# A decode step in one kernel: the last K ahead of two V, and W_o cut in other sets

## The chip, the cores and the metric

The kernel runs on one core of a Trainium2 chip. The metric is the device time of one execution in microseconds; the figure for a kernel is the median of several runs. The program works on five engines: TensorE (PE), VectorE (DVE), ScalarE (ACT), GpSimd (POOL) and SyncE (SP), which here issues the transfers. Sixteen DMA engines carry these transfers.

## The reference

One decode step for two sequences: attention over a cache of 8192 positions with 32 heads, then a gated feed-forward block, each behind a layer norm and with a residual sum.

```python
def _A_ref(x, k_cache, v_cache, wq, wo):
    q = (x @ wq).reshape(B, Sq, Hq, Dh).transpose(0, 2, 1, 3)
    scores = jnp.einsum("bhqd,bhkd->bhqk", q, k) * (Dh ** -0.5)
    p = softmax(scores, axis=-1)
    o = jnp.einsum("bhqk,bhkd->bhqd", p, v)
    return o.transpose(0, 2, 1, 3).reshape(B, Sq, Hq * Dh) @ wo

def _B_ref(x, W_gate, W_up, W_down):
    gate, up = x @ W_gate, x @ W_up
    return (gate * (gate > 0) * up) @ W_down

h = x + _A_ref(_layernorm(x), k_cache, v_cache, wq, wo)
h2 = h + _B_ref(_layernorm(h), W_gate, W_up, W_down)
```

B = 2, Sq = 1, D = 512, Hq = Hkv = 32, Dh = 128, 8192 cached positions, F = 1376, all bf16. The two caches are 128 MB each and are read once.

## The kernel before

**Steps.** The work runs in 32 steps; step i takes one sequence b and a group g of two heads. Each step loads 4 MB of K into one half of `kbuf` and 4 MB of V into one half of `vbuf` (half i % 2). A partition holds 128 positions of one head, partitions 0 to 63 head 0 and 64 to 127 head 1. In the text "K 31" is the K of step 31, and so on; the last step, 31, is called L in the changed code.

**Order by hand.** The whole kernel is in one manual schedule: each engine runs its instructions in program order, and waits are put in where a region of a buffer is still read or written. This holds for SP's queue of transfers too: a load that waits holds back every load behind it. Waits go by regions, so that a quarter of V can be issued when the matmuls that read that quarter are done. There are eight semaphores for transfers, used in turn: a transfer waits until the one eight places before it has landed.

**Scores.** In a step the 128 positions of a partition are shared out. VectorE takes 96 of them (80 in the last step): `products` (L338) multiplies K by q in place, `scores` (L353) adds halves down to a width of 8 and reduces (L357), then takes the maximum of a partition (L361). TensorE takes the other 32 (48 in the last step): `scores_pe` transposes eight tiles at a time (L311), ScalarE copies them out as `kT` (L313), and matmuls with q (L302) gather rows, which are copied (L318), transposed back (L321) and put into `scol` (L328). `largest` (L368) takes the maximum over partitions by a matmul, and `exponentials` (L380, L383) writes the weights into `pgz` and their sums into `zc`.

**Values.** `values(i, part)` multiplies the weights by V, 16 matmuls of 128x512 in each of two parts (L399), copies the result (L406), and where a group of heads ends, gathers it as `o_ps` (L411). `values_cols` does the same with V as the stationary operand (L423), 128 small matmuls. `sums`, `shares` and `normalise` divide by the sums of the exponentials and write `ocol`.

**Output projection.** W_o is 4 MB, in `wbig` behind the place of wq. Heads 0 to 26 are taken in three sets (`SETS`: first head, heads, partitions, place), loaded such that each partition holds whole rows of W_o: 16 heads and 8 heads on 128 partitions, 3 heads on 48. `spread` (L437, L442) lays the heads' outputs over these partitions, `attend_set` turns them into rows with `rest` (L456) and multiplies (L464). The last five heads go one by one with `attend` (L472), their W_o laid out by d. The set of 3 heads is loaded by two transfers of 24 partitions each, whose rows are named in the order `[[r*D, 6], [6*r*D, 4]]`. `spread` runs when a group of heads is finished: sets 0, 1 and 2 in steps 25, 29 and 31.

**The end.** After the loop come the last sums, `values_cols(31)`, five heads of `attend`, the residual sum `hc` (L541), the second layer norm, gate and up (L561) with weights that lie in `kbuf`'s first half, where K 30 was, and W_down (L588), whose chunks 0 to 7, 10, 8 and 9 are used in that order. The loads of gate, up and W_down are the last on SP's queue, behind the four quarters of V 31.

**Order of the last loads:** K 29, V 28, K 30, V 29, K 31, V 30, V 31 in four quarters, gate, up, W_down in three.

## Time and profile before

| | us |
|---|---|
| median of 3 runs | 665.12 (664.72 to 666.16) |
| the profiled execution | 664.74 |
| its span | 663.0 |
| TensorE busy | 489.4 (74%) |
| VectorE busy | 475.9 (72%) |
| ScalarE busy | 219.5 (33%) |
| transfers on SP's queue | 98.6% of 16 engines' span |

The profile is of one execution, and times in it count from the start of its span; the execution took 1.74 us more than the span. Three groups of instructions show what the engines wait for (name, count, busy time, mean of one in ns, then the idle time just before and what ended it):

```
L399 PE MATMUL pv_ps<-vbuf,pgz 128*8 128x512 bf16 x960 | 277.6, 455 | 66.6 <-DMA vbuf<-in_A_v_cache_dram 66.6
L338 DVE TENSOR_TENSOR kbuf<-kbuf,qrep 128x12288 bf16<-128x12288 bf16 (+1 forms) x32 | 208.8, 6525 | 107.9 <-DMA kbuf<-in_A_k_cache_dram 107.9
L313 ACT ACTIVATE kT<-t_ps 128x1024 bf16<-128x1024 bf16 x130 | 129.4, 1022 | 43.0 <-PE t_ps L311 40.9
```

Both TensorE and VectorE wait for V and K. A step lasts 19.4 us, two loads of 9.7 us.

### The profile page before, as it was taken

How to read it: one execution, taken by the hardware profiler on the slowest of the kernel's cores; microseconds unless marked ns; L12 is line 12 of the kernel's file. 1: busy time of each engine (PE TensorE's matmuls, PEld its weight loads, DVE VectorE, ACT ScalarE, POOL GpSimd, SP SyncE). 2: the span in 40 equal slices, each digit the busy share in tenths (PEclk: the TensorE clock that was granted, in tenths of full speed). 3: DMA queues.
4: the chain of work that ended last, by engine and by line, in shares of the span. 5: the costliest groups of instructions: out<-in, count | busy, mean ns of one | idle time of the engine just before them, and what ended most of it. 6: DMA issues, size and time to landing. Idle time of an engine off the chain costs nothing.

```text
span 663.0 us, 7717 instructions
## 1 busy us (share of the span) xinstructions
PE 489.4 (74%) x3282; PEld 229.2 (35%) x3282; DVE 475.9 (72%) x306; ACT 219.5 (33%) x400; POOL 17.8 (3%) x73
## 2 busy tenths in 40 slices
PE   3656777787777668787777867776877876788786
PEld 2422232333223333332333322333333432343266
DVE  0594788667778777778877767877777787776771
ACT  1532233333233333133333322333331333332250
POOL 8200000000000000000000000000000000000000
PEclk9968878988878998787899877899887888987785
DMA  9999999999999999999999999999999999999995
GB/s 380 431 413 445 424 443 428 427 439 430 429 436 437 426 441 427 427 440 431 430 435 428 434 433 432 429 434 437 426 435 438 422 435 438 431 432 432 433 417 202
DMA packets 11970, 281.58 MB, mean 425 GB/s; under 512 B 1518, under 2 KB 2288, under 8 KB 2672
## 3 DMA queue, kind: packets, MB, share of 16 engines
q1 hardware_dynamic: 11932, 281.09, 98.6%
q8 instruction: 25, 0.41, 0.2%
q14 instruction: 9, 0.07, 0.0%
q10 hardware_dynamic: 4, 0.00, 0.0%
HBM read 281.09 MB, written 0.00 MB: 424 GB/s over the span
## 4 chain that ended last, share of the span: by engine, by line
DMA 68%; PE 21%; DVE 9%; ACT 1%; issue 0%; SPq 0%; DVEq 0%; ACTq 0%
DMA vbuf<-in_A_v_cache_dram 53%; PE pv_ps L399 17%; DMA kbuf<-in_A_k_cache_dram 15%; DVE kbuf L353 4%; DVE kbuf L338 4%; PE o_ps L423 1%; PE mx_ps L368 1%; ACT kT L313 1%; DVE scol L357 1%; PE row_ps L302 0%; PE g_ps L561 0%; PE t_ps L311 0%; PE d_ps L588 0%; PE u_ps L561 0%; PE z_ps L268 0%
## 5 line engine op out<-in xcount | busy, mean ns | idle before, releaser
L399 PE MATMUL pv_ps<-vbuf,pgz 128*8 128x512 bf16 x960 | 277.6, 455 | 66.6 <-DMA vbuf<-in_A_v_cache_dram 66.6
L338 DVE TENSOR_TENSOR kbuf<-kbuf,qrep 128x12288 bf16<-128x12288 bf16 (+1 forms) x32 | 208.8, 6525 | 107.9 <-DMA kbuf<-in_A_k_cache_dram 107.9
L353 DVE TENSOR_TENSOR kbuf<-kbuf 128x6144 bf16<-128x6144 bf16 (+4 forms) x128 | 211.1, 1649 | 4.2
L399 PEld LDWEIGHTS <-pgz 128*8 128x8 bf16 x960 | 92.4, 99 | 227.8 <-issue 153.5
L313 ACT ACTIVATE kT<-t_ps 128x1024 bf16<-128x1024 bf16 x130 | 129.4, 1022 | 43.0 <-PE t_ps L311 40.9
L383 ACT ACTIVATE pgz<-scol,nm 64x128 bf16<-64x128 f32 x64 | 25.5, 399 | 263.0 <-DVE nm L380 262.2
L302 PE MATMUL row_ps<-kT,qz 128*16 128x512 bf16 (+1 forms) x260 | 78.5, 383 | 40.1 <-ACT kT L313 37.4
L311 PE MATMUL t_ps<-ident,kbuf 128*128 128x128 bf16 x1040 | 77.6, 225 | 10.6 <-DMA kbuf<-in_A_k_cache_dram 10.3
L311 PEld LDWEIGHTS <-kbuf 128*128 128x128 bf16 x1040 | 61.4, 101 | 51.1 <-issue 30.6
L302 PEld LDWEIGHTS <-qz 128*16 128x16 bf16 (+1 forms) x260 | 20.0, 87 | 63.2 <-issue 47.0
L406 ACT ACTIVATE pv<-pv_ps 8x512 f32<-8x512 f32 x30 | 17.6, 588 | 65.7 <-PE pv_ps L399 65.7
L380 DVE TENSOR_REDUCE nm<-mx_ps 128x2 f32<-128x128 f32 x32 | 9.3, 292 | 37.8 <-PE mx_ps L368 37.8
L357 DVE TENSOR_REDUCE scol<-kbuf 128x96 f32<-128x768 bf16 (+1 forms) x32 | 30.4, 949 | 1.1
L321 PE MATMUL sc_ps<-ident_f,rows 16*128 16x16 f32 (+1 forms) x128 | 13.4, 214 | 21.6 <-ACT rows L318 21.6
L318 ACT ACTIVATE rows<-row_ps 16x512 f32<-16x512 f32 (+1 forms) x32 | 18.8, 586 | 21.8 <-PE row_ps L302 21.8
L368 PE MATMUL mx_ps<-nscale,pm 128*128 128x128 f32 x64 | 16.2, 337 | 9.7 <-DVE pm L361 9.5
L321 PEld LDWEIGHTS sc_ps<-ident_f,rows 16*128 16x128 f32 (+1 forms) x128 | 10.3, 136 | 37.7 <-ACT rows L318 37.7
L328 ACT ACTIVATE scol<-sc_ps 64x32 f32<-64x32 f32 (+1 forms) x64 | 14.2, 223 | 17.0 <-PE sc_ps L321 16.2
L368 PEld LDWEIGHTS mx_ps<-nscale,pm 128*128 128x128 f32 x64 | 9.9, 195 | 23.4 <-DVE pm L361 16.0
L411 PE MATMUL o_ps<-pick,pv 128*128 128x8 f32 (+1 forms) x64 | 8.4, 258 | 5.5 <-ACT pv L406 5.5
L383 ACT ACTIVATION_READ_ACCUMULATOR pgz<-scol,nm 64x1 f32 x64 | 11.8, 185 | 0.0
L361 DVE TENSOR_REDUCE pm<-scol 128x1 f32<-128x128 f32 x32 | 9.2, 286 | 3.4 <-ACT scol L328 0.2
(91 smaller groups left out, 107.7 us busy)
## 6 DMA issues: line engine op xcount, KB each, us to landing
kbuf<-in_A_k_cache_dram SPq DMA_DIRECT2D x32, 4096.0 KB, 24.3
vbuf<-in_A_v_cache_dram SPq DMA_DIRECT2D x31, 4096.0 KB, 29.4
wbig<-in_A_wq_dram SPq DMA_DIRECT2D x1, 4096.0 KB, 12.1
vbuf<-in_A_v_cache_dram SPq DMA_DIRECT2D x4, 1024.0 KB, 18.2
wbig<-in_A_wo_dram SPq DMA_DIRECT2D x1, 2048.0 KB, 31.7
kbuf<-in_B_W_gate_dram SPq DMA_DIRECT2D x1, 1376.0 KB, 21.4
kbuf<-in_B_W_up_dram SPq DMA_DIRECT2D x1, 1376.0 KB, 24.2
wbig<-in_A_wo_dram SPq DMA_DIRECT2D x1, 1024.0 KB, 33.8
```

The lines of the kernel that those rows point to most:

```text
L302: nc.tensor.matmul(out=row_ps, lhsT=qz[:, b, g, z0:z0 + 2 * U], rhs=kTs[c0][:, k * P:(k + 4) * P], start=(u == 0), stop=(u == U - 1),)
L311: nc.tensor.transpose(t_ps[:, k, :], kt[:, t * Dh:(t + 1) * Dh], ident)
L313: nc.scalar.activation(out=kTs[c0], in_=t_ps.rearrange("p t s -> p (t s)"), func=ACT.Copy)
L318: nc.scalar.activation(out=rows, in_=row_ps, func=ACT.Copy)
L321: nc.tensor.transpose(sc_ps[:, t].rearrange("p u j -> p (u j)"), rows[:, t * P:(t + 1) * P], ident_f[0:2 * U, 0:2 * U],)
L338: nc.vector.tensor_tensor(out=kv, in0=kv, in1=_free(qrep, (b * NG + g) * Dh, [[0, nv], [1, Dh]]), op=ALU.mult,)
L353: nc.vector.tensor_tensor(out=lo, in0=lo, in1=_free(kt, half, [[Dh, nv], [1, half]]), op=ALU.add,)
L357: nc.vector.tensor_reduce(out=scol[:, 0:nv], in_=_free(kt, 0, [[Dh, nv], [1, 8]]), axis=AXIS.X, op=ALU.add,)
L368: nc.tensor.matmul(out=mx_ps.rearrange("p a b -> p (a b)"), lhsT=_free(pms[i], 0, [[0, P]]), rhs=nscale, start=True, stop=True,)
L383: nc.scalar.activation(out=pgz[r, s, :, j, :], in_=scol[r, :].rearrange("p (u t) -> p u t", t=VG), func=ACT.Exp, scale=SCALE, bias=nm[r, j ...
L399: nc.tensor.matmul(out=pv_ps[i][r, :], lhsT=pgz[:, s, u].rearrange("p j t -> p (j t)"), rhs=vbuf[:, s, u * VG * Dh:(u + 1) * VG * Dh], sta ...
L406: nc.scalar.activation(out=pv[r, w], in_=pv_ps[i][r, :], func=ACT.Copy)
```

## The change

Three things, in one diff:

- **Order of the last loads.** V 29 is no longer issued in step 28 but in step 29 behind K 31, in two halves; the order becomes K 29, V 28, K 30, K 31, V 29 in two, V 30, V 31 in four, gate, up, W_down in three. The loop ends one step sooner, and the last step is written out.
- **TensorE's share of step 31 in two parts.** `scores_pe` takes a range of tiles. Its first three groups run in step 30 behind `scores(30)`, the other three between the two parts of `values(29)`. Steps 30 and 31 use `values_cols`, each behind the exponentials of step 31; single heads are attended between its pieces.
- **W_o in other sets.** 16 heads on 128 partitions; 4 heads on 32 partitions, by two transfers of 16 partitions with rows named in the order `[[r*D, 4], [4*r*D, 4]]`; 4 heads on 128 partitions, kept in `wd_sb` where W_down comes later; the last 8 heads by d. Sets 1 and 2 are both worked in step 29. The memset of the unused partitions of set 2 is gone, and the input row x is kept in another chunk of `wd_sb`.

```diff
-    SETS = [(0, 16, P, 0), (16, 8, P, 16), (24, 3, 48, 32)]
-    WO_T = 24
-    HM = 27
+    SETS = [(0, 16, P, 0), (16, 4, 32, 16), (20, 4, P, 0)]
+    WO_T = 32
+    HM = 24
...
+    def wo_set(k):
+        at = SETS[k][3] * D
+        return wd_sb.rearrange("p c n -> p (c n)")[:, at:] if k == 2 else wbig[:, at:]
...
-        xr = wd_sb[0:B, 0, :]
+        xr = wd_sb[0:B, FC - 2, :]
...
-        nc.gpsimd.memset(wbig[0:HALF, SETS[2][3] * D:(SETS[2][3] + SROWS[2]) * D], 0.0)
...
-            part, rows = (P, [[r * D, P]]) if w == P else (24, [[r * D, 6], [6 * r * D, 4]])
+            part, rows = (P, [[r * D, P]]) if w == P else (16, [[r * D, 4], [4 * r * D, 4]])
...
-        def scores_pe(i):
+        def scores_pe(i, c1, c2):
...
-            for c0 in range(0, npe, TPC):
+            for c0 in range(c1, c2, TPC):
...
+            if c2 < npe:
+                return
...
                     nc.vector.tensor_copy(
-                        _free(placed, b * HALF, [[32, 2], [1, 4], [4, 6]]), _free(sp, 0, [[24, 2], [6, 4], [1, 6]]),
+                        _free(placed, b * HALF, [[32, 2], [1, 4], [4, 4]]), _free(sp, 0, [[16, 2], [4, 4], [1, 4]]),
                     )
...
-        def attend_set(k, sps, last=False):
+        def attend_set(k, sps):
...
-            p1 = P if w == P else HALF
+            p1 = P if w == P else 48
...
+        L = N - 1
+        for i in range(L):
             if i >= 2:
                 sums(i - 2)
+            scores_pe(i, 0, NPE)
             products(i)
+            ready = behind(i - 2) if i >= 2 else []
+            for k, sps in ready:
+                attend_set(k, sps)
+            if 1 <= i < L - 1:
                 values(i - 1, 0)
             scores(i)
+            if i == L - 1:
+                scores_pe(L, 0, NPE_LAST // 2)
             largest(i)
             exponentials(i)
             if i + 2 < N:
                 load_kv(A_k_cache, kbuf, i + 2)
+            if i == L - 2:
+                load_kv(A_v_cache, vbuf, i, pieces=2)
+            if 1 <= i < L - 1:
                 values(i - 1, 1)
+            if i + 1 < L and i != L - 3:
+                load_kv(A_v_cache, vbuf, i + 1)
...
+        products(L)
+        values(L - 2, 0)
+        scores_pe(L, NPE_LAST // 2, NPE_LAST)
+        values(L - 2, 1)
+        load_kv(A_v_cache, vbuf, L, pieces=4)
...
+        sums(L - 2)
+        scores(L)
+        behind(L - 2)
+        largest(L)
+        exponentials(L)
+        values_cols(L - 1)
+        for h in range(HM, 2 * (NG - 2)):
+            attend(h)
+        sums(L - 1)
+        behind(L - 1)
+        values_cols(L, 0, NT // 4)
+        sums(L)
+        shares(L)
+        values_cols(L, NT // 4, NT // 2)
+        for h in range(2 * (NG - 2), 2 * (NG - 1)):
+            attend(h)
+        values_cols(L, NT // 2, NT)
+        normalise(L)
+        for h in range(2 * (NG - 1), Hq):
             attend(h)
```

More of the change, by code (lines that the diff above doesn't have):

```diff
@@ L217 @@
                 nc.scalar.activation(out=qrep[:, b, g0:g0 + 4, :], in_=r_ps, func=ACT.Copy)
-        for (h0, n, w, at), r in zip(SETS, SROWS):
-            part, rows = (P, [[r * D, P]]) if w == P else (24, [[r * D, 6], [6 * r * D, 4]])
-            for k in range(w // part):
+        for k, ((h0, n, w, _), r) in enumerate(zip(SETS, SROWS)):
+            part, rows = (P, [[r * D, P]]) if w == P else (16, [[r * D, 4], [4 * r * D, 4]])
+            for j in range(w // part):
                 nc.sync.dma_start(
-                    out=wbig[32 * k:32 * k + part, at * D:(at + r) * D],
-                    in_=_dram(A_wo, (h0 * Dh + part * k * r) * D, rows + [[1, r * D]]),
+                    out=wo_set(k)[32 * j:32 * j + part, 0:r * D],
+                    in_=_dram(A_wo, (h0 * Dh + part * j * r) * D, rows + [[1, r * D]]),
                 )
@@ L285, in share @@
             return NT - npe, npe
-        def scores_pe(i):
+        rows_pe = {}
+        def scores_pe(i, c1, c2):
             b, g = steps[i]
-            s = i % 2
-            kt = kbuf[:, s, :]
+            kt = kbuf[:, i % 2, :]
             nv, npe = share(i)
             U = npe // 4
-            row_ps = ps.tile([2 * U, 4 * P], f32, tag="row")
-            kTs = {}
+            if c1 == 0:
+                rows_pe[i] = (ps.tile([2 * U, 4 * P], f32, tag="row", name="row_ps"), {})
+            row_ps, kTs = rows_pe[i]
             def times_q(c0):
@@ L323, in scores_pe @@
                 )
-            scol = small.tile([P, NT], f32, tag="scol")
-            scols[i] = scol
+            scols[i] = small.tile([P, NT], f32, tag="scol", name="scol")
             for j in range(2):
@@ L328, in scores_pe @@
                 nc.scalar.activation(
-                    out=scol[r, nv:NT].rearrange("p (u t) -> p t u", t=4), in_=sc_ps[r, :, :, j], func=ACT.Copy,
+                    out=scols[i][r, nv:NT].rearrange("p (u t) -> p t u", t=4), in_=sc_ps[r, :, :, j], func=ACT.Copy,
                 )
@@ L430, in spread @@
         def spread(k):
-            h0, n, w, at = SETS[k]
+            h0, n, w, _ = SETS[k]
             nq = Dh // SROWS[k]
@@ L442, in spread @@
                     nc.vector.tensor_copy(
-                        _free(placed, b * HALF, [[32, 2], [1, 4], [4, 6]]), _free(sp, 0, [[24, 2], [6, 4], [1, 6]]),
+                        _free(placed, b * HALF, [[32, 2], [1, 4], [4, 4]]), _free(sp, 0, [[16, 2], [4, 4], [1, 4]]),
                     )
-                    sp = placed[:, b, :]
+                    sp = placed[:, b, 0:48]
                 sps.append(sp)
             return sps
-        def attend_set(k, sps, last=False):
-            h0, n, w, at = SETS[k]
+        def attend_set(k, sps):
+            w = SETS[k][2]
             r = SROWS[k]
-            p1 = P if w == P else HALF
+            p1 = P if w == P else 48
             or_ps = ps.tile([P, B, r], f32, tag="mx")
@@ L456, in attend_set @@
                 nc.tensor.matmul(out=or_ps[0:p1, b, :], lhsT=sps[b], rhs=rest[k], start=True, stop=True)
-            o, i = orow[k][0:p1], or_ps[0:p1].rearrange("p b c -> p c b")
-            if last:
-                nc.vector.tensor_copy(o, i)
-            else:
-                nc.scalar.activation(out=o, in_=i, func=ACT.Copy)
+            nc.scalar.activation(out=orow[k][0:p1], in_=or_ps[0:p1].rearrange("p b c -> p c b"), func=ACT.Copy)
             for c0 in range(r):
@@ L465, in attend_set @@
                         out=att_ps[:, c, :],
-                        lhsT=_free(wbig[0:p1], (at + c0) * D + c, [[KC, P]]), rhs=orow[k][0:p1, c0, :],
+                        lhsT=_free(wo_set(k)[0:p1], c0 * D + c, [[KC, P]]), rhs=orow[k][0:p1, c0, :],
                         start=(k == 0 and c0 == 0 and c == 0), stop=False, skip_group_check=True,
@@ L488, in behind @@
             return ready
-        for i in range(N):
-            last = i == N - 1
+        L = N - 1
+        for i in range(L):
             if i >= 2:
                 sums(i - 2)
-            scores_pe(i)
+            scores_pe(i, 0, NPE)
             products(i)
-            if i >= 2 and not last:
-                for k, sps in behind(i - 2):
-                    attend_set(k, sps)
-            if last:
-                values_cols(i - 1, 0, NT // 2)
-            elif i >= 1:
+            ready = behind(i - 2) if i >= 2 else []
+            for k, sps in ready:
+                attend_set(k, sps)
+            if 1 <= i < L - 1:
@@ L502 @@
                 values(i - 1, 0)
             scores(i)
+            if i == L - 1:
+                scores_pe(L, 0, NPE_LAST // 2)
             largest(i)
-            ready = behind(i - 2) if last else []
             exponentials(i)
-            if last:
-                values_cols(i - 1, NT // 2, NT)
-                for k, sps in ready:
-                    attend_set(k, sps, last=True)
             if i + 2 < N:
                 load_kv(A_k_cache, kbuf, i + 2)
-            if 1 <= i < N - 1:
+            if i == L - 2:
+                load_kv(A_v_cache, vbuf, i, pieces=2)
@@ L514 @@
+            if 1 <= i < L - 1:
                 values(i - 1, 1)
-            if i + 1 < N:
-                load_kv(A_v_cache, vbuf, i + 1, pieces=4 if i + 1 == N - 1 else 1)
+            if i + 1 < L and i != L - 3:
+                load_kv(A_v_cache, vbuf, i + 1)
             if i == NG // 2:
                 nc.sync.dma_start(out=wd_sb[:, FC - 1, :], in_=_dram(B_W_down, FSETS[-1][0] * D, [[D, P], [1, D]]))
-            if i == N - 2:
-                for w, src in ((0, B_W_gate), (1, B_W_up)):
-                    nc.sync.dma_start(
-                        out=wgu[:, w], in_=_dram(src, 0, [[KC * F, P], [F, KC], [1, F]]),
-                    )
-                for f0, n in FSETS[:-1]:
-                    nc.sync.dma_start(
-                        out=wd_sb[:, f0 // P:f0 // P + n, :],
-                        in_=_dram(B_W_down, f0 * D, [[n * D, P], [1, n * D]]),
-                    )
@@ L529 @@
-        sums(N - 2)
-        shares(N - 2)
-        normalise(N - 2)
-        sums(N - 1)
-        shares(N - 1)
-        values_cols(N - 1)
-        normalise(N - 1)
-        for h in range(HM, Hq):
+        products(L)
[3 more added lines that the diff above has]
+        load_kv(A_v_cache, vbuf, L, pieces=4)
+        for w, src in ((0, B_W_gate), (1, B_W_up)):
+            nc.sync.dma_start(out=wgu[:, w], in_=_dram(src, 0, [[KC * F, P], [F, KC], [1, F]]))
@@ new lines @@
+        for f0, n in FSETS[:-1]:
+            nc.sync.dma_start(
+                out=wd_sb[:, f0 // P:f0 // P + n, :], in_=_dram(B_W_down, f0 * D, [[n * D, P], [1, n * D]]),
+            )
+        sums(L - 2)
[11 more added lines that the diff above has]
+        shares(L)
```

## The prediction

> **What bounds the kernel.** I read the page first, then the tail in narrow stretches, then SyncE's issues, then the chain of waits.

> ```profile
> span 663.0 us, 7717 instructions
> ...
> DMA  9999999999999999999999999999999999999995
> ...
> HBM read 281.09 MB, written 0.00 MB: 424 GB/s over the span
> ```

> The DMA engines are full from start to end and the bytes are the same after the change (W_o is cut differently, 4 MB both times). So only the last stretch can move: how far the sixteen DMA engines end apart, and what is computed after.

> ```profile
> 650.00:652.00 2.00, 2.00 (x78) 2.00 (x75) 0.16 (x1) 0.00 (x0) 0.00 (x0) 0.50 0.92 387
> 652.00:653.00 1.00, 0.74 (x12) 0.66 (x10) 0.17 (x1) 0.00 (x0) 0.00 (x0) 0.50 0.81 326
> 653.00:654.00 1.00, 0.54 (x13) 0.47 (x14) 0.57 (x4) 0.00 (x0) 0.00 (x0) 0.50 0.78 305
> 654.00:655.00 1.00, 0.59 (x19) 0.51 (x17) 0.00 (x0) 0.00 (x0) 0.00 (x0) 0.50 0.62 251
> 655.00:656.00 1.00, 1.00 (x27) 1.00 (x26) 0.00 (x0) 0.00 (x0) 0.00 (x0) 0.50 0.48 174
> 656.00:657.00 1.00, 1.00 (x34) 1.00 (x35) 0.69 (x5) 0.00 (x0) 0.00 (x0) 0.50 0.08 33
> 657.00:658.00 1.00, 1.00 (x37) 1.00 (x35) 0.32 (x3) 0.00 (x0) 0.00 (x0) 0.50 0.06 23
> ```

> The last two columns are the DMA share and GB/s. The engines stop one after another from 651 on, and from 657 the share is 0.06, one engine of sixteen. This straggler carries the last of W_down. I followed every packet of the trace engine by engine (a packet starts where the last of its engine ends) and took the sixteen completions of each load. The last W_down load completes at 651.44 to 651.64 on three engines, 653.94 to 654.44 on three, 655.63 to 656.12 on eight, 656.59 on one, 658.44 on the straggler.

> ```profile
> 641.14 1.70 PE o_ps L423 x64
> ...
> 645.61 1.20 PE att_ps L464 x32
> ...
> 648.24 3.41 PE o_ps L423 x128
> ...
> 657.46 1.50 PE d_ps L588 x44
> 658.96 0.02 issue
> 658.98 0.17 DVE y L593
> ```

> The chain says PE, but d_ps reads chunks 8 and 9 last, and they land at 658.44: y starts 0.54 us later (eight matmuls at 1.50/44 = 0.034, and the way to VectorE). Computation and straggler end together; shortening one gains nothing.

> ```profile
> 604.11 0.33 SPq L126 DMA_DIRECT2D kbuf<-in_A_k_cache_dram  x1
> 610.18 20.37 SPq L126 DMA_DIRECT2D vbuf<-in_A_v_cache_dram  x5
> 630.65 0.38 SPq L521 DMA_DIRECT2D kbuf<-in_B_W_gate_dram  x1
> ```

> K 31 is issued at 604.11, V 30 at 610.18, the quarters of V 31 at 623.33, 626.26, 628.50 and 630.23, each as soon as the values matmuls on that quarter are done.

> **Part 1, the order.** V 29 (issued 589.62, landed 619.68) goes behind K 31 (landed 629.35). They swap places: K 31 lands near 619.7, V 29 near 629.3. No byte is added; one more issue, 0.33 us on SP, is hidden by its 14 us waits. What is late next is the queue: between K 30's issue (584.16) and K 31's nothing waits on SP. The earliest engines finish K 30 at 602.6, so they run dry for 3 to 4 us. They end 7 us ahead of the straggler, so that costs nothing; if they had no such lead it would cost those 3 to 4 us.

> **Part 2, step 31 earlier.** The transposes of step 31 (632.01 to 641.14 before) are split: three groups while VectorE is in step 30, three between the halves of values(29). That delays values(29,1) and so the last two quarters of V 31, on SP behind it; gate, up and down too. Working forward: largest(30) ends near 626; values(29,0) 16 matmuls, half at 0.43 and half at 0.22, to 631; the second half of the transposes 9.1 - 3 x 1.13 = 5.7 to 637; values(29,1) 16 x 0.22 to 640.5. The quarters are then issued by 629, 631, 639 and 640.5; engines at mid field want the third at 639 to 641, so at most some of them idle 1 us. VectorE: products(31) 5.5, tree 5.7 and reductions 1.1 end near 638.5; it then waits for o_ps(29) (copy 0.6, eight matmuls 1.05) to 642, so exponentials(31) end near 644.7, as before (644.9). From the tail goes set 2 (0.21 + 0.17 + 1.20 us) and 12 of 20 last matmuls (0.4). V 31's last quarter lands at 648.75 as before, and half of values_cols (64 x 0.027 = 1.7) comes behind it or behind PE: hc near 652.0 against 652.36. Gain of computation: 0.35 us.

> **Part 3, W_o.** Set 1 becomes 64 matmuls, set 2 sixteen, in place of 32: 48 x 0.0375 = 1.8 us on PE in step 29, and four more VectorE operations of 0.2 us, hidden by PE's waits for V (2.8 us) and VectorE's for K (3.1 us); uncovered, 2.6 us. K 31's issue moves by about 0.8 us, more if K 29 lands later. The POOL memset (3.50 us) goes; PE waits for wq until 12.9 anyway: nothing.

> The DMA side matters more. The two 192 KB loads with an outer count of 6 ran on six engines only: each completed on six, and their 8 KB packets went to six. The new loads have an outer count of 4: I take four engines. Time per engine, start to start: 16 KB 0.608, 8 KB 0.306, 4 KB 0.157, 1 KB 0.0437 us. Before, behind set 0: 8 x 0.306 + 40 x 0.0437 = 4.20 on all and 8 x 0.306 more on six, 6.65. After: 8 x 0.157 + 64 x 0.0437 = 4.06 on all, and 8 x 0.608 more on four, 8.92. So +2.27 us on four engines, -2.59 on an engine that drops out of the six, -0.14 on the rest. An engine never catches up, as its queue is hardly ever empty: the offsets of t = 54 are still there at the end.

> Is the straggler among the four? It is one of the six: its 16 KB instruction fetches at 131, 379 and 603 cost it about 1.2 us each. The fetches of 16 KB go around eight engines in a fixed order; the other seven are all outside the six. The 8 KB fetches sit on four others of the six, and the sixth has none. Two neighbouring blocks, five engines and then eight, fit this: the six are the first block and the first engine of the second, the straggler is the last of them, and the four leave it out. But the trace names no engine; the other end fits too. Bounds: left out, it ends at 658.44 - 2.59 = 655.85, and the engine at 656.59 is last with 658.86; kept, 660.71.

> [...]

> [...]

> **Sum.** Straggler left out: last landing 658.86, y 0.54 later: 659.40 against 658.98, +0.42. The profiled execution took 664.74 (span 663.0 and 1.74 around it), 0.38 under the median of 665.12. Forecast 665.12 + 0.4 = 665.5, own range 664.6 to 666.4.

> **Rivals.** (a) The straggler is one of the four: +2.27, 667.4. For it: the straggler is one of the six, and four of six are kept; against: the order of fetches. It decides as soon as that engine is among those four, since nothing else ends after 658.86.
> (b) PE is late. If the clock is halved through values(29), as in 618.8 to 625.6, 16 matmuls cost 16 x 0.21 = 3.4 us more in the second half, and o_ps(29), the exponentials and hc are late by that: hc 652.0 + 3.4 = 655.4 against 652.36, +3.0, 668.1; with the other half of the first too, 1.7 more, 669.8. It decides once hc is over 0.8 us later than the 652.0 above. For it: little work on PE at 623 to 625; against: the clock was full while transposes ran, 605 to 618.
> (c) The loads spread over all engines, or the straggler's helpers differ: 512 KB in 16 KB packets is two per engine, 1.22, so the six go by 4.06 + 1.22 - 6.65 = -1.37 and the rest by +1.08: last landing 657.2. Then computation decides: between -0.35 and -1.24, 664.3. For it: nothing but that the four are not shown.

> **Chances.** Forecast 0.52, (a) 0.24, (b) 0.14, (c) 0.10. About 0.2% (1.3 us) is what can be told from no change. Of the forecast 0.03 falls faster (it costs the spans by single rows, and computation may end earlier than I put it) and 0.03 slower, of (b) 0.02 within, of (c) half faster: faster 0.08, same 0.46 + 0.02 + 0.05 = 0.53, slower 0.03 + 0.24 + 0.12 = 0.39. Range: from (c) below to (a) and 0.4 us of its own spread above, 664.3 to 667.8; most of (b) stays out, about 0.12.

> **What would show it.** The products of K 31 should start near 626 and not 629.4; hc near 652; the DMA share should fall to about 0.06 to 0.2 after 656 and end near 658.5 if the forecast holds, near 660.4 under (a). Under (b) the values matmuls of step 29 after 632 take 0.43. If y starts more than 1 us after the last landing, computation bounds the end and my part 2 is wrong; if the loads of set 1 complete on sixteen engines, part 3 is.

## The result and the profile after

The changed kernel takes 666.76 us (median of 9 runs, 666.04 to 668.14), the kernel before 664.77 us beside it: a ratio of 1.0026, 95% interval 1.0015 to 1.0037, that is 2.0 us more. The profiled execution took 667.58 us, its span is 665.9. It is one of the longer of the nine, 0.82 us over the median, so the profile shows a larger loss (2.8 us against the 664.74 of the profiled execution before) than the medians do.

The page of the changed kernel: span, the DMA engines' busy tenths, the packets that carry instructions (count, MB, share of 16 engines), and the rate.

```profile
span 665.9 us, 7791 instructions
...
DMA  9999999999999999999999999999999999999995
...
q8 instruction: 26, 0.43, 0.2%
...
HBM read 281.09 MB, written 0.00 MB: 422 GB/s over the span
```

The bytes are the same and the engines are as full as before. The next view cuts the end into stretches (length, busy time and instructions of TensorE, its weight loads, VectorE, ScalarE and GpSimd, then the granted clock, the DMA share and GB/s).

```profile
652.00:653.00 1.00, 0.35 (x14) 0.26 (x10) 0.00 (x0) 0.00 (x0) 0.00 (x0) 0.50 0.96 402
653.00:654.00 1.00, 0.00 (x0) 0.00 (x0) 0.00 (x0) 0.00 (x0) 0.00 (x0) 0.50 0.99 407
654.00:655.00 1.00, 0.20 (x2) 0.15 (x3) 0.16 (x1) 0.00 (x0) 0.00 (x0) 0.50 0.94 387
...
656.00:657.00 1.00, 0.54 (x12) 0.47 (x12) 0.57 (x4) 0.00 (x0) 0.00 (x0) 0.50 0.94 367
657.00:658.00 1.00, 1.00 (x39) 1.00 (x36) 0.00 (x0) 0.00 (x0) 0.00 (x0) 0.50 0.40 160
658.00:659.00 1.00, 1.00 (x27) 1.00 (x24) 0.33 (x2) 0.00 (x0) 0.00 (x0) 0.50 0.12 47
```

Two things are to be seen. The DMA share falls in one cliff after 657 where it fell slowly from 651 on before: the engines now end together, and late. And from 653 to 654 no engine computes at all, TensorE included, though V 31 had landed at 649.61. The chain of waits says for how long (start, duration, what):

```profile
646.74 0.24 PE o_ps L431 x9
646.98 1.36 issue
648.35 0.78 PE o_ps L431 x23
...
650.67 1.68 PE o_ps L431 x63
652.35 2.19 issue
654.54 0.20 PE o_ps L431
...
655.42 0.18 DVE hc L556
...
656.70 1.47 PE g_ps L576 x44
...
659.92 1.48 PE d_ps L603 x44
661.43 0.17 DVE y L608
```

The kernel before had one such wait on its chain, which the prediction passed over; it also stands at number 6337:

```profile
653.63 0.69 PE g_ps L561 x17
654.32 0.41 issue
654.73 0.96 PE g_ps L561 x27
```

The sixteen completions of the last load of W_down, in order of time:

```
before   651.44 651.60 651.64 653.94 654.38 654.44 655.63 655.78 655.78 655.86 655.89 655.97 655.98 656.12 656.59 658.44
changed  656.93 656.96 656.99 657.09 657.12 657.16 657.20 657.44 657.74 657.85 657.92 658.36 658.40 658.67 658.92 659.27
```

The spread of 7.0 us has become 2.3, but the last is 0.83 later. y starts 2.16 us behind it (0.54 before): the computation sets the end of this execution, and the loads stand close behind.

### The profile page after: what moved, and what is told of

Its sections match the earlier page's. It is cut to its first block, busy times and chain, and to the rows that moved or that the text cites. A ratio compares the mean times of both kernels' runs of the same rounds, so it can differ in the third digit from the quotient of the medians.

```text
span 665.9 us, 7791 instructions
## 1 busy us (share of the span) xinstructions
PE 486.9 (73%) x3310; PEld 229.5 (34%) x3310; DVE 475.6 (71%) x305; ACT 219.9 (33%) x401; POOL 16.0 (2%) x80
## 2 busy tenths in 40 slices
DMA  9999999999999999999999999999999999999995
## 3 DMA queue, kind: packets, MB, share of 16 engines
q1 hardware_dynamic: 12440, 281.09, 98.4%
HBM read 281.09 MB, written 0.00 MB: 422 GB/s over the span
## 4 chain that ended last, share of the span: by engine, by line
DMA 68%; PE 25%; DVE 5%; ACT 1%; issue 1%; SPq 0%; ACTq 0%; DVEq 0%
DMA vbuf<-in_A_v_cache_dram 61%; PE pv_ps L407 20%; DMA kbuf<-in_A_k_cache_dram 7%; DVE kbuf L361 2%; DVE kbuf L346 2%; PE mx_ps L376 1%; PE o_ps L431 1%; ACT kT L320 1%; PE row_ps L309 1%; PE t_ps L318 0%; DVE scol L365 0%; PE d_ps L603 0%; PE g_ps L576 0%; PE u_ps L576 0%; PE att_ps L476 0%
## 5 line engine op out<-in xcount | busy, mean ns | idle before, releaser
L407 PE MATMUL pv_ps<-vbuf,pgz 128*8 128x512 bf16 x960 | 270.2, 445 | 58.7 <-DMA vbuf<-in_A_v_cache_dram 58.7
L407 PEld LDWEIGHTS <-pgz 128*8 128x8 bf16 x960 | 90.7, 97 | 214.3 <-issue 135.7
L309 PE MATMUL row_ps<-kT,qz 128*16 128x512 bf16 (+1 forms) x260 | 80.8, 393 | 39.5 <-ACT kT L320 36.9
L318 PE MATMUL t_ps<-ident,kbuf 128*128 128x128 bf16 x1040 | 79.5, 228 | 15.9 <-DMA kbuf<-in_A_k_cache_dram 15.8
L318 PEld LDWEIGHTS <-kbuf 128*128 128x128 bf16 x1040 | 63.0, 102 | 57.8 <-issue 32.3
L309 PEld LDWEIGHTS <-qz 128*16 128x16 bf16 (+1 forms) x260 | 19.9, 88 | 63.3 <-issue 47.6
```

What stands on the lines that cost most here:

```text
L309: nc.tensor.matmul(out=row_ps, lhsT=qz[:, b, g, z0:z0 + 2 * U], rhs=kTs[c0][:, k * P:(k + 4) * P], start=(u == 0), stop=(u == U - 1),)
L318: nc.tensor.transpose(t_ps[:, k, :], kt[:, t * Dh:(t + 1) * Dh], ident)
L407: nc.tensor.matmul(out=pv_ps[i][r, :], lhsT=pgz[:, s, u].rearrange("p j t -> p (j t)"), rhs=vbuf[:, s, u * VG * Dh:(u + 1) * VG * Dh], sta ...
```

## Experiments

Three questions: do the waits come from the count of TensorE's instructions; which part of the change makes the last load later; and what does the loss go back to. Each run was timed beside the kernel before, on the same chip; the kernel before took 664.70 to 664.88 us there.

### Moving the borders: 64, 128 and 192 instructions more

The 32 transposes of step 4 (and 6, and 8) are made twice, where TensorE waits for K and V anyway (in the changed kernel in step 4 0.32 us for K and 2.83 for V, in step 6 0.81 and 2.84, in step 8 2.77 for V alone). Nothing else changes.

```diff
+        PAD = (4,)
...
-                    nc.tensor.transpose(t_ps[:, k, :], kt[:, t * Dh:(t + 1) * Dh], ident)
+                    for _ in range(2 if i in PAD else 1):
+                        nc.tensor.transpose(t_ps[:, k, :], kt[:, t * Dh:(t + 1) * Dh], ident)
```

> TensorE gets 64 more instructions long before the end (the 32 transposes of step 4 are made twice), which moves the borders of its 256-instruction blocks by 64 in what follows. Theory F (in the tail TensorE waits for its own instructions at each border): the two stalls of 1.36 and 2.19 us move to other matmuls, to 64 instructions earlier, in the second part of values_cols(30) and about 32 matmuls before the end of values_cols(31); the second is near 1.7 us; y starts near 660.6, the time falls by about 0.8 us against the changed kernel. Theory D (TensorE waits for V 31 or another engine there): the stalls stay in front of the same matmuls and the time is that of the changed kernel within 0.3 us.

> The transposes of steps 4 and 6 are made twice: the borders move by 128 instructions. Theory F: one stall of about 1.4 us is left, in values_cols(31) near its middle, none at its end; the residual sum is ready near 653 and the last landing (about 659.3) sets the end again: y some 0.55 us behind it, near 659.8, time 1.3 to 1.7 us below the changed kernel. Theory D: no change within 0.3 us, the stalls of 1.4 and 2.2 us at the same matmuls.

> The transposes of steps 4, 6 and 8 are made twice: the borders move by 192 instructions. Theory F: a stall of about 1.5 us in values_cols(31), none over 0.3 us behind it; y near 659.8, time 1.2 to 1.7 us below the changed kernel. Theory D: as the changed kernel, within 0.3 us.

Measured: 666.27, 666.38 and 666.24 us, ratios 1.0017 (1.0009 to 1.0026), 1.0022 (1.0013 to 1.0031) and 1.0021 (1.0012 to 1.0030). The wait stands again at number 6337 (0.75, 1.31 and 1.10 us from the end of one matmul to the start of the next), and in the third also at 6593 (0.34), though these numbers now fall 32, 64 and 96 matmuls (a weight load and a matmul each) earlier in the work. The chain with 64 more:

```profile
641.18 17.46 DMA wd_sb<-in_B_W_down_dram
658.64 0.05 issue
658.69 1.11 PE d_ps L605 x28
659.82 0.17 DVE y L610
```

The end is a transfer again, and y follows the last load (659.28) by 0.54 us, with the others by 0.58 and 0.56. So the waits belong to the number of the instruction, not to its data. But the time falls by only 0.4 to 0.5 us of the 2.0, not the 0.8 to 1.7 that were expected, and the intervals overlap that of the changed kernel (1.0015 to 1.0037): behind TensorE's waits stood the last load, at 659.28 to 660.21 against 658.44. So these runs show by the place, and not by the time, what the waits belong to.

### The order alone, W_o alone

First the new order of steps 28 to 31 with the sets of before; then the new sets with the order of before.

```diff
-    SETS = [(0, 16, P, 0), (16, 4, 32, 16), (20, 4, P, 0)]
-    WO_T = 32
-    HM = 24
+    SETS = [(0, 16, P, 0), (16, 8, P, 16), (24, 3, 48, 32)]
+    WO_T = 24
+    HM = 27
...
-        behind(L - 2)
+        ready = behind(L - 2)
...
         values_cols(L - 1)
+        for k, sps in ready:
+            attend_set(k, sps, last=True)
```

> The new order of the last steps with the W_o sets of before (16, 8 and 3 heads, 5 by d). Theory 'queues' (the end of the last load moves by what the W_o loads leave on single DMA engines, the order moves no engine's end): last load lands at 658.4 as before, y starts at 659.0 to 659.4, time 664.9 to 665.5. Theory 'order' (K 31 issued late lets engines run dry, and that is what makes the last load later): last load at 659.2, y 659.8, time 665.6 to 666.3. Theory 'blocks' (TensorE waits at instruction indices 193 + 256 n of its own stream): the count is that of before, 6575, so 6081 falls some 28 matmuls later than in the changed kernel, near the third quarter of step 31's values, 0.5 to 1 us, and 6337 inside g_ps, up to 0.5 us.

Measured: 664.96 us, 1.0003 (0.9994 to 1.0012). The last load lands at 658.28, and the one wait at a border is 0.44 us at 6081; the end of the chain:

```profile
638.19 19.47 DMA wd_sb<-in_B_W_down_dram
657.66 0.05 issue
657.71 1.11 PE d_ps L605 x28
658.84 0.17 DVE y L610
```

```diff
-        L = N - 1
-        for i in range(L):
+        for i in range(N):
+            last = i == N - 1
...
-            scores_pe(i, 0, NPE)
+            scores_pe(i, 0, share(i)[1])
...
+            if last:
+                values_cols(i - 1, NT // 2, NT)
+                for h in range(HM, 2 * (NG - 2)):
+                    attend(h)
```

> The new W_o sets (four heads on four engines, eight by d) with the order of before. Theory 'queues': last load lands at 658.9 to 659.3 as in the changed kernel, on one of the four engines; time 665.3 or more. Theory 'order': last load at 658.4. Theory 'blocks': 6631 instructions, so index 6337 falls about 8 matmuls before the end of step 31's values and costs 1 to 2 us there: hc near 654, y 659.8 to 660.4, time 665.6 to 666.5, near the changed kernel's 666.76. Without such a wait hc stays near 652.5 and y follows the last load by 0.54: 665.2 to 665.6.

Measured: 666.56 us, 1.0022 (1.0013 to 1.0031). The last load lands at 659.42, and the chain has

```profile
651.57 0.20 PE att_ps L476 x6
651.77 2.60 issue
654.37 0.48 PE att_ps L476 x10
654.87 0.18 DVE hc L546
...
659.39 1.48 PE d_ps L593 x44
660.89 0.17 DVE y L598
```

The order costs nothing that can be told, and the sets bring the whole loss: +1.86 of +1.99 us. They bring it in both ways, a later last load (+0.98) and a TensorE stream whose border at 6337 falls between the W_o matmuls. That place was put 14 matmuls too early; it is behind the sixth of the 16 that follow the last values. The completions of the last load lie between 654.53 and 658.28 with the order alone and between 653.40 and 659.42 with W_o alone. So it is the order that draws the engines together, and by holding up the early ones (651.44 to 651.64 before); the last is hardly sooner.

### No load on few engines

Sets of 16 and 8 heads on 128 partitions and eight heads by d, first with the order of before, then with the new one.

```diff
-    SETS = [(0, 16, P, 0), (16, 4, 32, 16), (20, 4, P, 0)]
-    WO_T = 32
+    SETS = [(0, 16, P, 0), (16, 8, P, 16)]
+    WO_T = 24
```

> No load on fewer than sixteen engines: sets of 16 and 8 heads on 128 partitions and eight heads by d, in the order of before. Theory 'queues': behind set 0 every engine has 8 x 0.306 + 64 x 0.0437 = 5.25 us, so the straggler of before gets 1.40 less (657.0) and the others 1.05 more (656.6 + 1.05 = 657.6): last load at 657.6, y 658.2 to 658.8, time 663.9 to 664.6. If the spread does not come from the W_o loads, the last load stays near 658.4 and the time near 664.9.

> The same sets as even8_before (16 and 8 heads on 128 partitions, eight by d) in the new order. Theory 'queues': last load at 657.6. Theory 'order': 658.4. Theory 'blocks': 6531 instructions, so index 6081 falls in the second 32 of step 31's values (about 1 us) and 6337 near the end of g_ps (up to 0.5 us): then y is set by TensorE at 658.8 to 659.4, time 664.5 to 665.3; without waits at blocks y is 658.2, time 663.9.

Measured: 664.92 us, 0.9999 (0.9990 to 1.0008), with the order of before; 664.50 us, 0.9992 (0.9984 to 1.0001), with the new order. The last load's completions:

```
old order, even sets  652.35 652.46 652.47 652.76 652.79 653.37 654.72 655.13 656.74 656.81 656.84 656.95 656.96 657.03 657.04 658.41
new order, even sets  654.87 654.94 654.98 655.01 655.15 655.15 655.17 655.65 656.77 656.83 657.02 657.10 657.11 657.18 657.24 657.31
```

In the new order all are in by 657.31, near the 657.6 of the sum. The waits at 6081 and 6337 are 0.84 and 0.58 us and cost nothing in the profiled execution (663.87, which is 0.63 us under the median), as its end is again a transfer, and y starts at 657.82, sooner than expected:

```profile
639.79 16.84 DMA wd_sb<-in_B_W_down_dram
656.62 0.05 issue
656.67 1.13 PE d_ps L603 x28
657.82 0.17 DVE y L608
```

In the old order fifteen engines are in by 657.04 and one at 658.41. A 16 KB instruction packet runs at 656.20 to 657.16 in that execution; that it sat on this engine fits the 1.4 us, but the trace names no engine. So that expectation of 663.9 to 664.6 was missed. Taking the four-engine loads out of the changed kernel gives 2.26 us back; as TensorE then has 100 instructions fewer, the borders move too, and the two effects are not parted here.

### Half of the few-engine load

Two heads in one load on four engines, six on 128 partitions; then the same with the 64 instructions more of the first experiment.

```diff
-    SETS = [(0, 16, P, 0), (16, 4, 32, 16), (20, 4, P, 0)]
+    SETS = [(0, 16, P, 0), (16, 2, 16, 16), (20, 4, P, 0), (18, 2, P, 4)]
...
-        return wd_sb.rearrange("p c n -> p (c n)")[:, at:] if k == 2 else wbig[:, at:]
+        return wd_sb.rearrange("p c n -> p (c n)")[:, at:] if k >= 2 else wbig[:, at:]
...
```

The lines left out drop `placed` and its memset and lay the heads of each set over as many partitions as the set has.

> Half of the few-engine load: two heads (16 to 17) on four engines in one load of 256 KB, heads 20 to 23 and 18 to 19 on 128 partitions, eight by d, new order. Theory 'queues': behind set 0 the four engines get 4 x 0.608 = 2.43 and all 8 x 0.157 + 8 x 0.083 + 64 x 0.0437 = 4.72 us; against the even sets (5.25) that is -0.53 on twelve and +1.90 on four. In the run with even sets the engines ended in two halves, near 655.0 and 656.8 to 657.3, and the four should be among the early half: last load at 656.8 to 657.0, the lowest of all. If the four are among the late half: 659.2. Theory 'blocks': 6651 instructions, so index 6337 falls 10 matmuls before the place it has in the changed kernel, still in step 31's last values: about 2 us, y near 660 to 661.4 whatever the loads do, time 666 to 667.3. Without waits at blocks y is 657.4 to 657.8, time 664.0 to 664.5.

> bal4 with the 32 transposes of step 4 made twice (64 instructions more, in a step where TensorE waits for K anyway): only the place of the blocks' borders moves. Theory 'blocks': index 6337 falls 42 matmuls earlier, as in the run with 64 instructions more (0.9 to 1.3 us there, before the last quarter), and 6593 behind g_ps: y follows the last load (656.8 to 657.0 by theory 'queues') by about 0.5: 657.4 to 657.9, time 664.0 to 664.5, that is 2 us and more under bal4. If the place of the borders doesn't matter, the two kernels take the same time.

Measured: 665.40 us, 1.0007 (0.9999 to 1.0016), and with 64 more 664.73 us, 0.9995 (0.9986 to 1.0004). The first stops at 6081 and 6337 (waits of 1.76 and 2.30 us), y at 659.44; the second only at 6337 (0.81), y at 658.50. Moving the borders gave 0.67 us and not 2, since the last load came at 657.86 and 657.94 and not at 656.9: half the load is better than all of it (659.27) and no better than none (657.31). The sum by engines gets the direction and is 1 us off here.

### The same set over sixteen engines

Two loads of 16 rows on 16 engines each, in place of 4 x 4 rows on four, with the heads' outputs laid over the partitions in the same order; later one load of 32 rows into 32 neighbouring partitions. The cut of the first:

```diff
-            part, rows = (P, [[r * D, P]]) if w == P else (16, [[r * D, 4], [4 * r * D, 4]])
+            part, rows = (P, [[r * D, P]]) if w == P else (16, [[r * D, 16]])
...
```

> The two loads of the set of four heads name their 16 rows in one dimension, and the heads' outputs are laid over the partitions in that order: the loads should complete on sixteen engines and not on four, and TensorE's instructions are the same. Theory F: the stalls stay where they are with 1.4 and 2.2 us, or the fetches are quicker by some tenths; the last landing falls from 659.3 to about 658.4 and y still comes over 1 us behind it, so that the time falls by 0 to 0.6 us. Rival E (the four late engines set the end): the time falls by as much as the last landing, 0.8 us or more, and y starts 0.55 us behind the landing.

> The changed kernel with set 1 as one load of 32 rows of 16 KB into 32 neighbouring partitions (outer count 32: two rows per engine), where the run with 16 rows per load (sixteen engines into 16 partitions at a time) had its 16 KB packets at up to 2.6 us instead of 0.61 and everything behind 4.9 us later. If what slows is the number of partitions written at a time (16 x 16 KB in 2.55 us, 103 GB/s into 16 partitions), the 16 KB packets take about 1.3 us and the last load lands at 658.4 to 659; if any sixteen-engine load of such rows crawls, 2.5 us and 661 or later; if neither, 0.61 us and 657.3. The waits at 6081 and 6337 stay as in the changed kernel (6631 instructions).

Measured: 671.65 us, 1.0099 (1.0085 to 1.0112), for the first, 4.9 us over the changed kernel, and 668.16 in a single run of the second. Both theories of the first were wrong. Its stretches around the W_o loads:

```profile
44.00:48.00 4.00, 3.50 (x17) 1.20 (x14) 3.97 (x2) 2.10 (x3) 0.00 (x0) 0.68 1.34 324
48.00:52.00 4.00, 3.40 (x19) 1.58 (x20) 3.93 (x3) 0.99 (x3) 0.00 (x0) 1.00 0.64 96
```

and those of the second:

```profile
48.00:52.00 4.00, 3.32 (x19) 1.53 (x19) 3.93 (x3) 1.03 (x3) 0.00 (x0) 1.00 0.95 209
```

In the changed kernel the last column has 386 there. With 16 rows per load a 16 KB packet takes up to 2.60 us, with 32 rows up to 1.70 and mostly 1.1 to 1.5, on four engines 0.61. As was expected, 32 partitions halve it: 16 x 16 KB in 2.55 us are 103 GB/s into 16 partitions, in 1.43 us 183 GB/s into 32. Four engines bring 4 x 16 KB in 0.61 us, 107 GB/s. So here the loads into 16 partitions went no faster on sixteen engines (103) than on four (107), and held up twelve more of them. What sets these rates no run shows; the number of partitions written at a time alone does not, as the four engines have only four such packets under way.

The last load of the second run (661.21) is later than expected (658.4 to 659); why is open.

### The kernel before with 64 instructions more

The cleanest test of the blocks: no load and no order is changed.

```diff
-                    nc.tensor.transpose(t_ps[:, k, :], kt[:, t * Dh:(t + 1) * Dh], ident)
+                    for _ in range(2 if i == 4 else 1):
+                        nc.tensor.transpose(t_ps[:, k, :], kt[:, t * Dh:(t + 1) * Dh], ident)
```

> The kernel before with the 32 transposes of step 4 made twice: the same loads, the same order, 64 TensorE instructions more in a step where it waits for K. Theory 'blocks': index 6337 falls 32 matmuls earlier, from the 17th of g_ps to the 7th of the last 20 W_o matmuls (651.9). The block is asked for at the crossing of 6081 (about 648.5) and comes 5.2 to 6.2 us later, 653.7 to 654.7: a wait of 1.8 to 2.8 us, hc at 654.2 to 655.2 and not 652.36, y 6.0 behind hc at 660.2 to 661.2: time 665.9 to 667.0, with the last load where it was (658.4). Rival: the waits of the changed kernel have to do with its own order or loads; then 64 instructions in step 4 do nothing: 664.5 to 665.0.

Measured: 665.91 us, 1.0014 (1.0005 to 1.0023).

```profile
651.11 0.23 PE att_ps L473 x7
651.35 1.94 issue
653.28 0.60 PE att_ps L473 x13
653.91 0.18 DVE hc L542
...
658.44 1.48 PE d_ps L589 x44
659.94 0.17 DVE y L594
```

The wait is behind the seventh of 20, as counted, and lasts 1.94 us; the last load lands at 658.15. Thirty-two transposes made twice, some 550 us before the end, in a step where TensorE waits 2.84 us for V (before) and not for K, cost 1.1 us, with the loads no later than before (658.44). The rival is out.

## Why the prediction was right or wrong

**Part 1, the order: right.** K 31 landed at 620.08 (forecast 619.7), and the order alone costs nothing that can be told (664.96). The engines ran dry as forecast: from 600 to 610 the DMA share is 0.94, with the order alone 0.97, before 1.00. K 31 was issued 2.0 us later and not 0.8. That comes with the sets, not with the order: it is issued at 606.10, at 606.59 with W_o alone, and at 603.90 with the order alone (604.11 before).

**Part 2, the times of step 31: right but for one term.** The products of K 31 started at 626.22 (forecast 626), values(29,1) ended at 639.9 (640.5), the exponentials at 644.0 (644.7). Then "hc near 652.0" failed: 655.42. The difference is the two waits, 1.36 + 2.19 = 3.55; without them hc would be at 651.9. The sum costed every instruction and not the supply of instructions. "If y starts more than 1 us after the last landing, computation bounds the end and my part 2 is wrong": 2.16.

These traces show blocks of 256 instructions, and waits at their borders in this tail of 0.41 us before, of 1.36 and 2.19 us in the changed kernel and of up to 2.60 us in the runs.

**Part 3, the engines: right in kind, too small in size.** The two loads complete on four engines, with four packets of 16 KB under way from 47.6 on, most of 0.61 us. Followed packet by packet, as far as that can be done where the trace names no engine, the straggler of before is not among them and its last packet ends at 657.6; the last engine is one of the four, and its last packet ends at 658.97. A load's completion stands some 0.3 us behind the last packet (658.10 and 658.44 before), so the forecast completions of 655.85 and 658.86 compare with about 657.9 and with the measured 659.27. That the four lie inside the six, as the sum takes it in its -2.59, was the author's assumption; no run shows it, as the traces name no engine. What they show are the two last packets, at 657.6 for the straggler and at 658.97 for one of the four. The term "+0.42" measured +0.83 here, +0.98 with W_o alone, and +0.84 to +1.77 with the borders moved.

The term that failed is the "-0.14 on the rest". In the packet records of the changed kernel twelve packets of 32 KB, as many as there are engines beside the four, start between 50.9 and 52.0, as the second load on four engines ends (51.46 to 52.09), and take 1.75 to 2.86 us where such packets take 1.22: 1.27 us more on average. From 52 to 54 the transfers run at 260 GB/s, before at 398. The same twelve stand in the run with W_o alone (1.92 to 2.84) and in that with 64 instructions more (2.07 to 2.90). With half the load there are seven, up to 1.72, and with 64 instructions more five, up to 2.21; in the kernel before, with the order alone and with even sets no packet of 32 KB takes over 1.3 us there. So the four-engine loads held up other engines as well. The completions agree: the eight that stood at 655.63 to 656.12 were to come a little sooner, and with W_o alone ten stand at 656.26 to 658.08. Why the chip slows these packets is not shown. The 0.41 us by which the last of the four is late on the forecast were not taken apart either; instruction packets, each some 0.9 us long, fall elsewhere once TensorE's count changes, and the sum kept them where they were.

**The sum.** Forecast +0.4, measured +2.0: above the forecast's own 666.4, and in the wide range by luck, since its upper part was there for (a). Two terms were missing, the waits for instructions and the packets held up. The runs with moved borders leave 1.4 to 1.5 us to the loads and 0.4 to 0.6 to TensorE's waits, the latter within the noise of these runs. They don't add: the later one of the two sets y. Alone, the waits cost 1.1 us (the kernel before with 64 instructions more) and the loads about 1.4 to 1.5.

**The rivals.** (a) did not happen. (c) did not either: four engines, not sixteen. (b)'s price came true in hc (655.42, 655.4 forecast) by chance, through another mechanism: the granted clock was 1.00 through values(29,1) (636.3 to 639.9), 3.56 us for 16 matmuls as forecast.

## What to carry to other kernels

When an engine shows a wait for nothing in the middle of equal instructions, count its instructions: here the waits stood at 6081 and 6337, 256 apart, and 64 instructions more, made far earlier, put number 6337 32 matmuls earlier in the work and the wait with it. It is worth placing such a wait where the engine waits anyway. Compare two versions of a tail only with this in mind, since a change of 56 instructions (6575 to 6631) shifts the borders as much as it shifts the work. A load on few engines is worth a look at their ends: here the transfers took 98.4% of the sixteen engines' span, one of the four came last (its last packet ended at 658.97, and the last load landed at 659.27, with even sets in the new order at 657.31), and the loads also held up twelve packets of other engines once, 1.75 to 2.86 us in place of 1.22, so their cost was more than the bytes on the few.

## What the hardware showed unexpectedly

- Where two borders in a row make TensorE wait, it starts again 6.2 us (changed kernel, and even sets in the new order), 5.9 (sixteen rows, thirty-two, and 192 instructions more) and 6.5 us (half the load) behind the start of the block before, while 256 instructions of these small matmuls take 3.4 us (128 weight loads and 128 matmuls in 3.41, in the kernel before). So in these runs the blocks of such matmuls ran out. Whether the fetch is this slow because the engines are full was not tried.
- As the two loads on four engines ended, twelve packets of 32 KB took 1.75 to 2.86 us in place of 1.22; with half the load seven took 1.35 to 1.72.
- Rows of 16 KB went into 16 partitions at 103 to 107 GB/s, on four engines and on sixteen, and into 32 partitions at 183 GB/s.
- The best version measured, even sets in the new order, is level with the kernel before within its interval (0.9984 to 1.0001).
